# Gated mix of attention and mlp on one core: the mlp in 32-row tiles, in two phases

## The chip, the core and the metric

The kernel runs on 1 core of one Trainium2 chip. The metric is the device time of one execution in microseconds (us). Five engines work beside each other, each with its own queue that it goes through in order: TensorE (PE; its weight loads are listed as PEld), VectorE (DVE), ScalarE (ACT), GpSimd (POOL) and SyncE (SP), which here only starts transfers. Matrix products go to PSUM banks of 128 partitions x 512 float32 numbers.

## The reference

Attention and an mlp of the same input are mixed by a gate for each row; S = 2048 rows, D = 448 columns, 16 heads of 28, 1792 hidden columns, float32.

```python
qkv = (x @ wqkv).reshape(1, S, 3, 16, 28).transpose(2, 0, 3, 1, 4)
q, k, v = qkv
p = softmax(einsum("bhqd,bhkd->bhqk", q, k) * 28 ** -0.5)
a = einsum("bhqk,bhkd->bhqd", p, v).transpose(0, 2, 1, 3).reshape(1, S, D) @ wo
y = (x - mean(x)) / sqrt(var(x) + 1e-5)
b = gelu_tanh(y @ w1 + b1) @ w2 + b2
g = sigmoid((x * gate_w).sum(-1))
out = g * a + (1 - g) * b
```

## The kernel before

Float32 accuracy comes from splitting: a number is a high part (rounded to the type fp32r) and a low part, the difference, and a product is three matmuls: high x high, high x low, low x high. S is cut into NC = 4 chunks of CH = 512 rows or 16 tiles of 128 rows (TPC = 4 a chunk); heads into NG = 4 groups of four; the hidden columns into NF = 14 tiles of 128.

The stages run one after the other. First q, k and v are computed and stored to DRAM (qk holds high and low parts). Then comes the mlp, then attention, then the last projection and the output.

The mlp goes over s = c, f (chunk, hidden tile; line 400). `mlp1(c, f)` adds 11 matmuls of 128 rows into one bank ph (line 368: K is 448, padded to four tiles, the low part of y sharing the fourth), ACT applies the gelu twice (lines 373 and 374: rounded and not), POOL subtracts to get the low part hl (line 375). `mlp2` of the step before adds its three products into four banks, one for each 128 rows (lines 385, 386, 388), that live over all 14 hidden tiles. Finished rows go to DRAM (gbs). So PE alternates between 11 matmuls of 512 columns and 12 of 448.

Attention subtracts the row maximum of the scores. These maxima come from matmuls of their own: q and k high parts of one head stand in 28 of the 32 rows of a strip of TensorE's array, four heads in four strips (kd, qd). Each matmul (line 280) gives 128 x 512 scores, each is reduced by DVE (line 282); 1024 of them are needed. `Filler` spreads them: 394 between the mlp's matmuls, in groups of MG = 3, the others (aux) through attention. For every 64 a PE transpose (line 264) and a store to ms follow.

For attention, K tiles (`load_k`: one transfer of ones, line 331, and two of 224 KB, line 338) and q tiles (`load_q`) are started on SP's queue; the first 12 K tiles go into the space of the mlp's w1 tiles (ring kring, name w1f). Their start is written into the mlp loop, in chunk 3 behind f = 10. A slot of attention is one K tile of 128 rows against 512 rows of q for four heads: four score matmuls (line 528), two exponentials on ACT (line 531), then p times v of the slot before (line 536: four matmuls, each in its own strip of 32 columns of the array, with full float32 operands; the profile lists eight), and some row maxima. `finish` divides by the sums: the sums go out and back by POOL's queue (lt, rls, rc) and the projection is added to acc. Before that, POOL loads acc from gbs and scales it by 1 - g (lines 515, 517, 518).

The order in each queue is set by a scheduler that follows the program's order and the waits of each instruction; a transfer on SP may so be put ahead of or behind others.

Of the kernel before, what the change touches and what calls it, by code (L numbers as in the profile page):

```python
# [15 lines left out]
P = 128  # L16
# [14 lines left out]
MLP_MAX = 400  # L31
MG = 3
FS = 3
# [5 lines left out]
def kernel(ctx: ExitStack, tc: tile.TileContext, xt, wqk, wv, wo, xk, w1, b1, w2, b2,  # L39
# [18 lines left out]
    ms = [dram.tile([4, S], F32, name=f"ms{g}") for g in range(NG)]  # L58
# [11 lines left out]
    mpool = ctx.enter_context(tc.tile_pool(name="mpool", bufs=2, side="right"))  # L70

    aq = ctx.enter_context(tc.tile_pool(name="aq", bufs=1, side="right"))


    m0 = ExitStack()
    mw0 = m0.enter_context(tc.tile_pool(name="mw0", bufs=1, side="right"))
    my = m0.enter_context(tc.tile_pool(name="my", bufs=2, side="right"))

    w1h, w1l, w2h, w2l = {}, {}, {}, {}
    kring = []  # L80
    qring = [aq.tile([P, 4, CH], F32R, name=f"qst{i}") for i in range(3)]

    def load_w(f, pool1, pool, stage):
        r1 = stage.tile([P, 4, P], F32, name="r1")
        nc.sync.dma_start(r1, w1[f])
        t = pool1.tile([P, 8, P], F32R, name=f"w1f{f}")
        w1h[f], w1l[f] = t[:, 0:4], t[:, 4:8]
        if f >= 2:
            kring.append(t.rearrange("p a b -> p (a b)"))
        nc.scalar.activation(w1h[f], r1, AF.Copy)  # L90
        nc.gpsimd.tensor_sub(w1l[f], r1, w1h[f].bitcast(F32))
        r2 = stage.tile([P, D], F32, name="r2")
        nc.sync.dma_start(r2, w2[f])
        w2h[f] = pool.tile([P, D], F32R, name=f"w2h{f}")
        w2l[f] = pool.tile([P, D], F32R, name=f"w2l{f}")
        nc.scalar.activation(w2h[f], r2, AF.Copy)
        nc.gpsimd.tensor_sub(w2l[f], r2, w2h[f].bitcast(F32))

    yh, yl, lnr, lnx = {}, {}, {}, {}

    def ln_load(c, t):
        cs = slice(c * CH, (c + 1) * CH)
        if t == 0:
            lnr[c] = my.tile([P, 2, CH], F32, name="lnr", bufs=1)
            nc.sync.dma_start(lnr[c], lns.rearrange("(n t) i -> n (t i)", n=2)[:, cs].partition_broadcast(P))
        lnx[c, t] = my.tile([P, CH], F32, name="xr", bufs=4)
        nc.sync.dma_start(lnx[c, t], xt[t, :, cs])

    def ln_apply(c, t):
        if t == 0:  # L110
            yh[c] = qring[c % 2]
            yl[c] = my.tile([P, 3, CH], F32R, name="yl")
        x = lnx.pop((c, t))
        nc.vector.tensor_sub(x, x, lnr[c][:, 0])
        nc.gpsimd.tensor_mul(x, x, lnr[c][:, 1])
        nc.scalar.activation(yh[c][:, t], x, AF.Copy)
        if t < 3:
            nc.vector.tensor_sub(yl[c][:, t], x, yh[c][:, t].bitcast(F32))
        else:
            nc.vector.tensor_sub(yh[c][64:128, t], x[64:128], yh[c][64:128, t].bitcast(F32))  # L120


    with tc.tile_pool(name="qx", bufs=2) as qx, tc.tile_pool(name="qo", bufs=3) as qo, \
# [85 lines left out]
        for c in range(NC):  # L209
            for m in range(NM):  # L210
# [23 lines left out]
                if c == 2 and m in (3, 5):  # L234
                    load_w(m // 4, mw0, mw0, my)
                if c == 2 and m == 6 or c == 3 and m < 3:
                    ln_load(0, (m + 1) % 7)
                if c == 3 and m in (1, 2, 3, 4):
                    ln_apply(0, m - 1)
# [5 lines left out]
    def row_max(pool):  # L245

        kds, qds = {}, {}

        def load(n):
            g, c = divmod(n, NC)  # L250
            if c == 0:
                kds[g] = mpool.tile([P, S], F32R, name="kd")
                for j in range(4):
                    r = D + (4 * g + j) * DH
                    pool[1].dma_start(kds[g][32 * j:32 * j + DH].bitcast(F32), qk[0, r:r + DH])
            qds[n] = mpool.tile([P, CH], F32R, name="qd")
            for j in range(4):
                r = (4 * g + j) * DH
                pool[1].dma_start(qds[n][32 * j:32 * j + DH].bitcast(F32), qk[0, r:r + DH, c * CH:(c + 1) * CH])

        def close(n, mf):
            g, c = divmod(n, NC)
            ps = pool[0]()
            nc.tensor.transpose(ps[:4 * TPC, :P], mf, ident)
            mt = mpool.tile([4 * TPC, P], F32R, name="mt")
            nc.vector.tensor_scalar(mt, ps[:4 * TPC, :P], -1.0, None, op0=OP.mult)
            pool[1].dma_start(ms[g][:, c * CH:(c + 1) * CH].rearrange("j (i x) -> j i x", x=P), mt.bitcast(F32))

        load(0)
        last = None  # L270
        for n in range(NG * NC):
            kd, qd = kds[n // NC], qds[n]
            mx = mpool.tile([P, 4, TPC, 4], F32, name="mx")
            done = 0
            for i in range(TPC):
                for k in range(4):
                    for j in range(4):
                        ps = pool[0]()
                        r = slice(32 * j, 32 * j + DH)
                        nc.tensor.matmul(ps, qd[r, i * P:(i + 1) * P], kd[r, k * 512:(k + 1) * 512],  # L280
                                         start=True, stop=True)
                        nc.vector.reduce_max(mx[:, j, i, k:k + 1], ps, axis=AX)  # L282
                        done += 1
# [3 lines left out]
                        if done == 24 and n + 1 < NG * NC:  # L287
                            load(n + 1)
# [332 lines left out]
```

## Time and profile before

| what | us |
|---|---|
| time before, median of 2 runs | 1273.99 (1272.26 to 1275.72) |
| span of the profiled execution | 1271.2 |
| q, k, v, to about | 118 |
| mlp, from about 118 to | 503 |
| from the mlp's end until attention runs without a stop | 503 to 603 |
| attention | 603 to 1232 |
| last projection and output | 1232 to 1271.2 |

The profile is of one execution. A page gives busy times of the engines and the costliest groups of instructions; a timeline lists them one by one; windows give busy times for stretches; the chain of waits follows the end back to what it waited for. PE's ends are modelled: the distance from one start to the next says more than the length.

### The profile page before, as it was taken

The page shows a single profiled execution, that of the slowest core. Times are in us where ns is not written, and L with a number is a line of the kernel's source. Part 1 is how long each engine was busy: PE and PEld are TensorE (multiplying, and loading weights), DVE is VectorE, ACT ScalarE, POOL GpSimd, SP SyncE. Part 2 cuts the span into 40 slices and gives each one's busy share as a digit, 9 for nine tenths or more (in the row PEclk, how much of TensorE's full clock was granted, in tenths as well). Part 3 has the DMA queues.
Part 4 walks back from the last instruction along what each step waited for, and adds up shares of the span by engine and source line. Part 5 has one row for each costly group of instructions (what it writes and reads, how often), then busy time and mean ns, then how long its engine had stood idle before and what let it go on. Part 6 is the DMA issues. An engine that isn't in the chain of part 4 may idle for free.

```text
span 1271.2 us, 16167 instructions
## 1 busy us (share of the span) xinstructions
PE 1196.9 (94%) x6085; PEld 653.2 (51%) x6085; DVE 775.9 (61%) x1298; ACT 645.0 (51%) x765; POOL 322.5 (25%) x362
## 2 busy tenths in 40 slices
PE   7998999999999998196999999999999999999997
PEld 6886667766677665032444434444434444444433
DVE  3543377877776776144676757666756777676703
ACT  5243522212212211164677757767657767767784
POOL 4022952311222112356222121112022202211220
PEclk9999899999999999588999989999989999999998
DMA  8987740100101212532013142102412111210001
GB/s 281 295 279 261 203 108 25 46 9 1 37 16 47 72 53 82 147 112 59 17 40 75 53 103 78 38 10 56 99 64 61 44 31 38 76 35 34 25 24 58
DMA packets 56053, 101.44 MB, mean 80 GB/s; under 512 B 7352, under 2 KB 24240, under 8 KB 55528
## 3 DMA queue, kind: packets, MB, share of 16 engines
q1 hardware_dynamic: 41640, 82.53, 21.0%
q0 software_dynamic: 6016, 13.70, 4.0%
q10 hardware_dynamic: 8320, 4.19, 1.5%
q8 instruction: 48, 0.79, 0.3%
q14 instruction: 29, 0.24, 0.1%
HBM read 73.76 MB, written 26.49 MB: 79 GB/s over the span
## 4 chain that ended last, share of the span: by engine, by line
PE 75%; DMA 14%; POOL 5%; issue 2%; DVE 2%; ACT 1%; SPq 1%; ACTq 0%; POOLq 0%; DVEq 0%
PE sc L528 20%; PE pv L536 17%; PE ph L368 11%; PE aux L280 7%; PE pm L280 5%; PE acc L388 4%; PE acc L385 4%; PE acc L386 3%; DMA w1f<-qk 3%; DMA lt<-ob 2%; DMA xraw<-in_xt 2%; DMA acc<-gbs 2%; POOL acc L518 1%; PE ps L160 1%; PE aux L454 1%
## 5 line engine op out<-in xcount | busy, mean ns | idle before, releaser
L531 ACT ACTIVATE pt<-sc 128x1024 f32<-128x1024 f32 x512 | 496.5, 1021 | 230.6 <-PE sc L528 219.8
L282 DVE TENSOR_REDUCE mx<-aux 128x1 f32<-128x512 f32 x630 | 396.2, 683 | 176.8 <-PE aux L280 176.3
L528 PE MATMUL sc<-qst,w1f 113*128 113x512 f32 x1024 | 317.5, 429 | 33.9 <-ACT pt L531 33.9
L282 DVE TENSOR_REDUCE mx<-pm 128x1 f32<-128x512 f32 x394 | 248.1, 684 | 92.0 <-PE pm L280 91.6
L536 PE MATMUL pv<-pt,vg 128*32 128x512 f32 x2048 | 279.3, 617 | 0.0
L528 PEld LDWEIGHTS sc<-qst,w1f 113*128 113x128 f32 x1024 | 172.7, 191 | 152.5 <-ACT pt L531 83.6
L373 ACT ACTIVATE hh<-ph,b1s 128x512 fp32r<-128x512 f32 x56 | 38.4, 686 | 247.5 <-PE ph L368 247.5
L368 PE MATMUL ph<-qst,w1f 128*128 128x512 f32 x448 | 152.2, 413 | 7.1 <-ACT h L374 7.0
L280 PEld LDWEIGHTS aux<-kd,qd 28*128 28x128 f32 x630 | 45.0, 184 | 199.6 <-DVE mx L282 123.6
L375 POOL TENSOR_TENSOR hl<-h,hh 128x512 fp32r<-128x512 f32 x56 | 73.1, 1305 | 245.6 <-ACT h L374 244.3
L280 PE MATMUL aux<-kd,qd 28*128 28x512 f32 x630 | 116.7, 503 | 14.5 <-DVE mx L282 14.3
L368 PEld LDWEIGHTS ph<-qst,w1f 128*128 128x128 f32 x448 | 84.3, 192 | 34.3 <-issue 11.0
L536 PEld LDWEIGHTS pv<-pt,vg 128*32 128x32 f32 x2048 | 40.8, 108 | 92.5 <-issue 86.1
L388 PE MATMUL acc<-w2h,hl 128*128 128x448 f32 x224 | 87.2, 389 | 0.0
L385 PE MATMUL acc<-w2h,hh 128*128 128x448 f32 x224 | 84.5, 377 | 0.0
L386 PE MATMUL acc<-w2l,hh 128*128 128x448 f32 x224 | 82.0, 366 | 0.0
L465 POOL DMA_DIRECT2D lt<-ob x15 | 10.7, 716 | 254.3 <-DVE ob L464 254.3
L280 PE MATMUL pm<-kd,qd 28*128 28x512 f32 x394 | 73.5, 497 | 1.2 <-DVE mx L282 0.4
L368 PE MATMUL ph<-yl,w1f 128*128 128x512 f32 x168 | 69.5, 414 | 0.0
L455 DVE SCALAR_TENSOR_TENSOR acc<-aux,gate,acc 128x448 f32<-128x448 f32 x64 | 43.4, 678 | 39.3 <-PE aux L454 39.3
L280 PEld LDWEIGHTS pm<-kd,qd 28*128 28x128 f32 x394 | 28.2, 182 | 48.8 <-DVE mx L282 36.0
L160 PE MATMUL ps<-xh,wh 128*128 128x512 f32 x112 | 45.5, 406 | 7.0 <-ACT xh L147 6.4
(99 smaller groups left out, 980.8 us busy)
## 6 DMA issues: line engine op xcount, KB each, us to landing
qk<-hl SPq DMA_DIRECT2D x28, 512.0 KB
qst<-qk SPq DMA_DIRECT2D x64, 224.0 KB
w1f<-qk SPq DMA_DIRECT2D x64, 224.0 KB
xraw<-in_xt SPq DMA_DIRECT2D x16, 256.0 KB
vs<-vt SPq DMA_DIRECT2D x16, 256.0 KB
xr<-in_xt SPq DMA_DIRECT2D x16, 256.0 KB
rc<-rls POOLq DMA_DIRECT2D x60, 64.0 KB, 2.3
bxr<-in_xk SPq DMA_DIRECT2D x8, 448.0 KB
```

Source lines behind the costliest of these rows:

```text
L160: nc.tensor.matmul(ps, a, b, start=(i == 0), stop=(i == len(ops) - 1))
L280: nc.tensor.matmul(ps, qd[r, i * P:(i + 1) * P], kd[r, k * 512:(k + 1) * 512], start=True, stop=True)
L282: nc.vector.reduce_max(mx[:, j, i, k:k + 1], ps, axis=AX)
L368: nc.tensor.matmul(ps, a, b, start=(i == 0), stop=(i == len(ops) - 1))
L375: nc.gpsimd.tensor_sub(hl[c, f], h, hh[c, f].bitcast(F32))
L385: nc.tensor.matmul(a, hh[c, f][:, sl], w2h[f], start=(f == 0), stop=False)
L386: nc.tensor.matmul(a, hh[c, f][:, sl], w2l[f], start=False, stop=False)
L388: nc.tensor.matmul(a, hl[c, f][:, sl], w2h[f], start=False, stop=(f == NF - 1))
L455: nc.vector.scalar_tensor_tensor(acc[:, tt], po, gate[:, tt:tt + 1], acc[:, tt], op0=OP.mult, op1=OP.add)
L528: nc.tensor.matmul(ps[:, i], kst[g, j, h][:4 * DH + 1, kk * P:(kk + 1) * P], qst[g, c][:4 * DH + 1, j], start=True, stop=True)
L531: nc.scalar.activation(t, ps, AF.Exp, scale=SCALE)
L536: nc.tensor.matmul(pv[32 * j:32 * j + 32, :], vg[g][:, k, 32 * j:32 * j + 32], pt[j // 2][:, j % 2], start=(k == 0), stop=(k == NT - 1), s ...
```

## The change

The mlp is written anew. Every matmul of it has 32 rows, one strip of the array. An item of work, `Up` (one hidden tile of a chunk) or `Down` (one tile of 128 output rows), has one PSUM bank and passes through the strips in turn: an `Up` spends one step in each strip (42 matmuls in all), a `Down` four turns of the four strips (168 matmuls). In each step a new item may begin in strip 0, so that up to four are in flight, each in another strip and another bank; one round of a step is one matmul from each. There are 123 steps (`NC * (NF + 16) + 3`).

Where the banks move on by a strip, SP waits for the last matmul of each and increments the semaphore hand, and PE waits for that. Ahead of the wait PE has three row maxima (`visit`, into three banks with one reduction by DVE) and the first matmul of a new item.

In each chunk all 14 ups come first (steps 0 to 16 of 30), then the four downs (14 on): hidden values hh, hl are kept for all 14 tiles, one buffer each. w1 and w2 are loaded one tile per step in the first chunk. The order of all engines in this loop is fixed as it is written; attention's first loads (`attention_early`) start at step 108 (in the last chunk, one step after its last up is done), one K tile a step, into tiles of their own in the space of w1.

Row maxima: kd has one buffer instead of two, each strip is reloaded by itself; the transposes are 32 x 32 on DVE instead of PE; ms has another layout. 369 row maxima are done in the mlp, 655 in attention. Attention is otherwise as before, with a third q tile outside the ring of the mlp's.

```diff
-MLP_MAX = 400
-MG = 3
-FS = 3
...
-    ms = [dram.tile([4, S], F32, name=f"ms{g}") for g in range(NG)]
+    ms = [dram.tile([32, 4, 32], F32, name=f"ms{n}") for n in range(NG * NC)]
...
+    def split_w1(f, eng):
+        r = w1r.pop(f)
+        t = w1s[f] = w1p[0].tile([P, 7, P], F32R, name=f"w1f{f}")
+        lo = slice(64 * ((f + 1) % 2), 64 * ((f + 1) % 2) + 64)
+        nc.scalar.activation(t[:, 0:4], r, AF.Copy)
+        eng.tensor_sub(t[:, 4:7], r[:, 0:3], t[:, 0:3].bitcast(F32))
+        eng.tensor_sub(t[lo, 3], r[lo, 3], t[lo, 3].bitcast(F32))
...
+    yh = aq.tile([P, 4, CH], F32R, name="yh")
+    yl = aq.tile([P, 4, CH], F32R, name="yl")
...
+            self.kd = mpool.tile([P, S], F32R, name="kd")
+            self.qd = [mpool.tile([P, CH], F32R, name=f"qd{i}") for i in range(2)]
...
+        def load_k(self, g, j):
+            r = D + (4 * g + j) * DH
+            self.queue.dma_start(self.kd[32 * j:32 * j + DH].bitcast(F32), qk[0, r:r + DH])
...
+        def visit(self, ps, count):
+            self.flush()
+            first = self.m
+            count = min(count, 64 * NG * NC - first)
+            for b in range(count):
+                n, x = divmod(self.m, 64)
+                x, j = divmod(x, 4)
+                i, k = divmod(x, 4)
+                if x == 0 and n + 1 < NG * NC:
+                    self.load_q(n + 1, j)
+                r = slice(32 * j, 32 * j + DH)
+                nc.tensor.matmul(ps[:, b], self.qd[n % 2][r, i * P:(i + 1) * P], self.kd[r, k * 512:(k + 1) * 512],
+                                 start=True, stop=True)
+                if x == 15 and n % NC == NC - 1 and n + 1 < NG * NC:
+                    self.load_k(n // NC + 1, j)
+                self.m += 1
+            if count:
+                nc.vector.reduce_max(self.mx[:, first % 192:first % 192 + count], ps[:, :count], axis=AX)
+            if self.m // 64 > first // 64:
+                self.late.append(lambda: self.close(first // 64))
...
+            mf, mt = self.mf[n % 2], self.mt[n % 2]
+            mx = self.mx[:, 64 * (n % 3):64 * (n % 3) + 64].rearrange("p (i k j) -> p j i k", i=TPC, k=4)
+            nc.vector.reduce_max(mf[:, 0:16].rearrange("p (j i) -> p j i", j=4), mx, axis=AX)
+            nc.vector.tensor_scalar(mf[:, 0:16], mf[:, 0:16], -1.0, None, op0=OP.mult)
+            nc.vector.transpose(mt, mf)
+            def store():
+                self.queue.dma_start(ms[n].rearrange("c b x -> b c x"), mt)
+            self.later.append(store)
...
-        t = qring[(0, 2, 1)[nq % 3]]
+        t = qring[nq % len(qring)]
...
+    mp = m1.enter_context(tc.tile_pool(name="mp", bufs=5, space=PSUM, reuse_waits="tile"))
+    mr = m1.enter_context(tc.tile_pool(name="mr", bufs=1, space=PSUM, reuse_waits="tile"))
...
+    class Up:
+        def __init__(self, c, f):
+            self.c, self.f, self.phases = c, f, 4
+        def ops(self, n):
+            f, w = self.f, w1s[self.f]
+            r = slice(32 * n, 32 * n + 32)
             ops = []
             for t in range(3):
-                ops += [(w1h[f][:, t], yh[c][:, t]), (w1h[f][:, t], yl[c][:, t]), (w1l[f][:, t], yh[c][:, t])]
-            ops += [(w1h[f][:, 3], yh[c][:, 3]), (w1l[f][:, 3], yh[c][:, 3])]
-            for i, (a, b) in enumerate(ops):
-                nc.tensor.matmul(ps, a, b, start=(i == 0), stop=(i == len(ops) - 1))
-                filler.run(1, MG)
+                ops += [(w[r, t], yh[r, t]), (w[r, t], yl[r, t]), (w[r, 4 + t], yh[r, t])]
+            ops.append((w[r, 3], yh[r, 3]))
+            if n // 2 == f % 2:
+                ops.append((w[r, 3], yl[r, 3]))
+            return ops
+        def close(self):
+            f = self.f
             h = mh.tile([P, CH], F32, name="h", bufs=2)
-            hh[c, f] = mh.tile([P, CH], F32R, name="hh")
-            hl[c, f] = mh.tile([P, CH], F32R, name="hl")
-            nc.scalar.activation(hh[c, f], ps, AF.Gelu_apprx_tanh, bias=b1s[:, f:f + 1])
-            nc.scalar.activation(h, ps, AF.Gelu_apprx_tanh, bias=b1s[:, f:f + 1])
-            nc.gpsimd.tensor_sub(hl[c, f], h, hh[c, f].bitcast(F32))
-        acc2 = {}
-        def mlp2(c, f):
-            for i in range(TPC):
-                if f == 0:
-                    acc2[c, i] = mp2.tile([P, D], F32, name="acc2")
-                sl = slice(i * P, (i + 1) * P)
-                a = acc2[c, i]
-                nc.tensor.matmul(a, hh[c, f][:, sl], w2h[f], start=(f == 0), stop=False)
-                nc.tensor.matmul(a, hh[c, f][:, sl], w2l[f], start=False, stop=False)
-                filler.run(2, MG)
-                nc.tensor.matmul(a, hl[c, f][:, sl], w2h[f], start=False, stop=(f == NF - 1))
-                filler.run(1, MG)
-                if f == NF - 1:
-                    tt = c * TPC + i
-                    gb = mh.tile([P, D], F32, name="gb", bufs=2)
-                    if c < NC - 1:
-                        nc.scalar.activation(gb, a, AF.Copy)
-                    else:
-                        nc.vector.tensor_copy(gb, a)
-                    (nc.sync if c < NC - 1 else nc.gpsimd).dma_start(gbs[tt], gb)
-        prev = None
-        for s in range(NC * NF):
-            c, f = divmod(s, NF)
-            if c == 0 and f + 2 < NF:
-                load_w(f + 2, ak, mw, my)
-            if s == FS:
-                filler.spread(lambda: mp3.tile([P, 512], F32, name="pm"), nc.sync, MLP_MAX, (NC * NF - FS) * 23)
-            mlp1(c, f)
-            if prev is not None:
-                mlp2(*prev)
-            prev = (c, f)
-            if c == NC - 1 and f == 10:
-                for j in range(4):
-                    load_k(0, j, 0)
-                load_q(0, 0)
-                for j in range(4):
-                    load_k(0, j, 1)
-            if 1 <= f < 5 and c + 1 < NC:
-                ln_load(c + 1, f - 1)
-            if f >= 6 and f % 2 == 0 and c + 1 < NC:
-                ln_apply(c + 1, (f - 6) // 2)
-        mlp2(*prev)
-    m0.close()
+            nc.scalar.activation(hh[f], self.ps, AF.Gelu_apprx_tanh, bias=b1s[:, f:f + 1])
+            nc.scalar.activation(h, self.ps, AF.Gelu_apprx_tanh, bias=b1s[:, f:f + 1])
+            nc.gpsimd.tensor_sub(hl[f], h, hh[f].bitcast(F32))
+    class Down:
+        def __init__(self, c, i):
+            self.c, self.i, self.phases = c, i, 16
+        def ops(self, n):
+            v, s = divmod(n, 4)
+            r = slice(32 * s, 32 * s + 32)
+            sl = slice(self.i * P, (self.i + 1) * P)
+            cut = ((0, 11, 21, 32, 42), (0, 10, 21, 31, 42))[self.i % 2]
+            ops = []
+            for m in range(cut[v], cut[v + 1]):
+                f, p = divmod(m, 3)
+                ops.append(((hh, hh, hl)[p][f][r, sl], (w2h, w2l, w2h)[p][f][r]))
+            return ops
+        def close(self):
+            gb = mh.tile([P, D], F32, name="gb", bufs=2)
+            nc.scalar.activation(gb, self.ps[:, :D], AF.Copy)
+            nc.sync.dma_start(gbs[self.c * TPC + self.i], gb)
...
+    def extra(t):
+        c, x = divmod(t, NF + 16)
+        if c == 0:
+            if x + 3 < NF:
+                fetch_w1(x + 3)
+            if x + 2 < NF:
+                split_w1(x + 2, nc.gpsimd if x < 6 else nc.vector)
+            if 8 <= x < 8 + NF:
+                fetch_w2(x - 8)
+            if 9 <= x < 9 + NF:
+                split_w2(x - 9)
+        if c + 1 < NC:
+            if 20 <= x < 24:
+                ln_load(c + 1, x - 20)
+            if 22 <= x < 26:
+                ln_sub(c + 1, x - 22)
+            if 23 <= x < 27:
+                ln_split(c + 1, x - 23)
+    def attention_early():
+        m0.close()
+        ak = ctx.enter_context(tc.tile_pool(name="ak", bufs=1, side="right", reuse_waits="tile"))
+        kring.extend(ak.tile([P, 2 * CH], F32R, name=f"kst{i}") for i in range(NK))
+        for j in range(4):
+            load_k(0, j, 0)
+            yield
+        load_q(0, 0)
+        yield
+        for j in range(4):
+            load_k(0, j, 1)
+            yield
...
+    starts = {}
+    for c in range(NC):
+        for f in range(NF):
+            starts[c * (NF + 16) + f] = Up(c, f)
+        for i in range(TPC):
+            starts[c * (NF + 16) + NF + i] = Down(c, i)
+    hand = tc.alloc_semaphore("hand")
+    handed = 0
+    over = []
+    handoff = mybir.DependencyInfo(mybir.DependencyClass.Sync, mybir.DependencyReason.DATA)
+    with tc.manual_schedule():
+        rowmax.begin()
+        live = []
+        early = None
+        for t in range(NC * (NF + 16) + 3):
+            if t in starts:
+                starts[t].n = 0
+                live.append(starts[t])
+            if t == (NC - 1) * (NF + 16) + NF + 4:
+                early = attention_early()
+            if early is not None:
+                next(early, None)
+            todo = [[] for _ in range(4)]
+            for x in live:
+                s = x.n % 4
+                if x.n == 0:
+                    x.ps = mp.tile([P, CH], F32, name="acc")
+                ops = x.ops(x.n)
+                last = x.n == x.phases - 1
+                for m, (a, b) in enumerate(ops):
+                    todo[s].append((x, a, b, x.n == 0 and m == 0, last and m == len(ops) - 1))
+                x.n += 1
+            rowmax.visit(mr.tile([P, 3, 512], F32, name="pm"), 3)
+            if todo[0] and todo[0][0][3]:
+                x, a, b, st, sp = todo[0].pop(0)
+                nc.tensor.matmul(x.ps[:, :b.shape[-1]], a, b, start=st, stop=sp, skip_group_check=True)
+            if over:
+                sig = nc.sync.sem_inc(hand, 1)
+                for mm in over:
+                    tc.add_manual_dep(sig.ins, mm.ins.name, handoff, reason="handoff")
+                handed += 1
+                nc.tensor.wait_ge(hand, handed)
+                over = []
+            while any(todo):
+                for s in range(4):
+                    if not todo[s]:
+                        continue
+                    x, a, b, st, sp = todo[s].pop(0)
+                    n = b.shape[-1]
+                    mm = nc.tensor.matmul(x.ps[:, :n], a, b, start=st, stop=sp, skip_group_check=True)
+                    if not todo[s] and x.n < x.phases:
+                        over.append(mm)
+            for x in [x for x in live if x.n == x.phases]:
+                x.close()
+                live.remove(x)
+            extra(t)
...
-    filler.spread(aux, nc.gpsimd, NG * NC * 65, (NG * NC - 2) * NT + LQ - 1)
+    rowmax.queue = nc.gpsimd
+    qring.append(aw.tile([P, 4, CH], F32R, name="qst2"))
+    first, slots, slot = rowmax.m, (NG * NC - 2) * NT + LQ - 4, 0
...
-                filler.run(1, 3)
+                slot += 1
+                if rowmax.m == 1024:
+                    rowmax.flush()
+                if rowmax.m < 1024 and first + (1024 - first) * min(1, slot / slots) - rowmax.m >= min(3, 1024 - rowmax.m):
+                    for _ in range(3):
+                        if rowmax.m < 1024:
+                            rowmax.visit(aux().rearrange("p (b n) -> p b n", b=1), 1)
```

More of the change, by code (lines that the diff above doesn't have):

```diff
@@ L79 @@
[L79 to L97, printed above, removed]
@@ L295 @@
-    class Filler:
-        def __init__(self):
-            self.pool = [None, None]
-            self.it = row_max(self.pool)
-            self.first = self.upto = self.slot = self.done = 0
-            self.slots = 1
-        def spread(self, pool, queue, upto, slots):
-            self.pool[:] = pool, queue
-            self.first, self.upto, self.slots, self.slot = self.done, upto, slots, 0
-        def run(self, n=1, group=1):
-            self.slot += n
-            due = self.first + (self.upto - self.first) * min(1, self.slot / self.slots) - self.done
-            group = min(group, self.upto - self.done)
-            if due >= group:
-                for _ in range(group):
-                    next(self.it, None)
-                    self.done += 1
@@ L321 @@
+    rowmax = RowMax()
     HS = S // 2
@@ L424, in sb @@
+    m1.close()
     def sb(name, bufs):
```

138 lines of the change are left out of this document (65 added, 73 removed).

## The prediction

> **What bounds the kernel now.** The page comes first: who is busy, and how long the execution was.
>
> ```profile
> span 1271.2 us, 16167 instructions
> PE 1196.9 (94%) x6085; PEld 653.2 (51%) x6085; DVE 775.9 (61%) x1298; ACT 645.0 (51%) x765; POOL 322.5 (25%) x362
> ```
>
> TensorE (PE) looks like the only bound, but 94% is an average over stages, so the windows come next (columns: stretch, length, busy time of PE, PEld, DVE, ACT, POOL, granted clock, DMA share, GB/s).
>
> ```profile
> 170.00:503.00 333.00, 333.00 (x1530) 232.58 (x1530) 245.19 (x399) 74.22 (x120) 77.82 (x68) 1.00 0.13 40
> 503.00:545.00 42.00, 8.09 (x28) 3.10 (x30) 4.73 (x11) 6.55 (x8) 15.34 (x16) 0.58 0.52 143
> 545.00:603.00 58.00, 46.82 (x260) 17.87 (x252) 29.75 (x49) 33.61 (x35) 35.44 (x31) 0.88 0.30 82
> 603.00:1232.00 629.00, 623.35 (x3473) 261.92 (x3473) 413.92 (x686) 438.88 (x453) 118.62 (x179) 0.98 0.19 51
> ```
>
> The mlp (to 503 us) and the attention (from 603 us) leave PE no gap. Between them lies a hole of two halves, and the change touches both sides of it. The chain of waits says what made it (start, length, what):
>
> ```profile
> 507.65 33.24 DMA w1f<-qk
> ...
> 550.70 10.42 DMA acc<-gbs
> 561.19 2.25 POOL acc L517 x2
> ...
> 597.48 2.72 POOL acc L518 x2
> 600.20 2.22 DMA lt<-ob
> ...
> 603.30 1.98 PE aux L280 x3
> ```
>
> First the K tiles of attention have to land, about 541 us; then PE does some twenty attention slots until it needs the first division, whose small transfer (lt) stands on POOL behind the initialisation of acc from the stored mlp rows: 561 to 600 us. So a shorter mlp is worth its gain only if K loads and that POOL chain also come earlier. Their order decides this case.
>
> **Part 1, the matmuls.** PE's timeline in the middle of the mlp (start, length, group):
>
> ```profile
> 299.65 0.39 PE L368 MATMUL ph<-qst,w1f 128*128 128x512 f32 x1
> 299.88 0.40 PE L368 MATMUL ph<-yl,w1f 128*128 128x512 f32 x1
> ...
> 302.15 0.86 PE L368 MATMUL ph<-qst,w1f 128*128 128x512 f32 x3
> 302.94 0.50 PE L280 MATMUL pm<-kd,qd 28*128 28x512 f32 x3
> 303.37 0.47 PE L385 MATMUL acc<-w2h,hh 128*128 128x448 f32 x1
> 303.68 0.37 PE L386 MATMUL acc<-w2l,hh 128*128 128x448 f32 x1
> 303.88 0.36 PE L388 MATMUL acc<-w2h,hl 128*128 128x448 f32 x1
> ```
>
> Starts are 0.23 us apart at 512 columns and 0.20 us at 448. Three row maxima, on three strips at once, hold the next full matmul off for 0.43 us (302.94 to 303.37), and that one takes 0.31 instead of 0.20 (to 303.68); before them 302.15 + 3 x 0.23 = 302.84, 0.10 us early. A triple costs 0.43 + 0.11 + 0.10 = 0.64 us, and of 394 row maxima there are 131 triples: 84 us of the mlp.
>
> The Trainium skill's page "TensorEngine Tiling (Array Packing)", section Key Properties, says that changing the tiling mode drains TensorE; the 0.43 and 0.31 us agree, and by that rule an mlp in 32-row tiles throughout pays no drain at a triple.
>
> After the change a step has 10 or 11 rounds of four strip matmuls. Strip matmuls: 56 ups x 42 and 16 downs x 42 x 4, together 5040, or 1260 rounds where there were 616 + 672 = 1288 full matmuls: the stream saved is only 28 x 0.22 = 6 us, if a round goes at the cadence of one full matmul. No row of before shows four row strips back to back. The near bound is 0.23 us (a strip reads only its own 32 partitions); the far one the four-wide packing by columns:
>
> ```profile
> 552.44 1.06 PE L536 MATMUL pv<-pt,vg 128*32 128x512 f32 x8
> 553.43 0.50 PE L280 MATMUL aux<-kd,qd 28*128 28x512 f32 x3
> ```
>
> Eight of these take 0.99 us, 0.50 us a round of four. There each strip pulls its own 128-partition stream, where row strips share one, and the operands are full float32 instead of fp32r. So I take 0.23, and keep 0.50 as the far end.
>
> **Part 2, the hand-over.** At each of 122 steps PE waits until the last matmul on every bank is done, by way of SP. What such a wait costs is bounded by how late ACT sees a bank finished, and by a wait's own length on PE's queue:
>
> ```profile
> 303.05 0.69 ACT L373 ACTIVATE hh<-ph,b1s 128x512 fp32r<-128x512 f32 x1 [5.01 <-PE ph L368]
> L528 PEldq EVENT_SEMAPHORE  x54: 51/51/1697, 499.4 to 1215.8; - x54
> ```
>
> The last ph starts at 302.15 + 2 x 0.23 = 302.61, ACT at 303.05: 0.44 us. With two hops of 51 ns, 0.54 us from the last round's start to the next round's; the row-max triple and one first matmul lie inside. With 11 rounds a step is 10 x 0.23 + 0.54 = 2.84 us (up) or 10 x 0.20 + 0.54 = 2.54 us (down). From below: without the wait 11 x 0.23 = 2.53. From above: another 0.4 us for SP, 3.2.
>
> Does something else bound a step? One reduction covers three banks:
>
> ```profile
> L282 DVE TENSOR_REDUCE mx<-pm x394: 669/681/694, 143.7 to 500.5; 128x1 f32<-128x512 f32 x197
> L375 POOL TENSOR_TENSOR hl<-h,hh 128x512 fp32r<-128x512 f32 x56 | 73.1, 1305 | 245.6 <-ACT h L374 244.3
> ```
>
> Three at 0.68 are 2.04 us if nothing is shared; the next triple waits for it, and 0.53 + 2.04 = 2.57 fits the step, barely in the down phase. POOL has 1.3 us per up beside weight splits; its cover is thin only in the first steps.
>
> The count: 17 up steps and 13 down-only steps a chunk. K loads are released when the last up is done, after 107 steps: 68 x 2.84 + 39 x 2.54 = 292 us. The first step now begins with row maxima, whose kd loads are late on SP:
>
> ```profile
> 127.40 0.41 SPq L255 DMA_DIRECT2D kd<-qk  x1
> ...
> kd<-qk POOLq DMA_DIRECT2D x8, 224.0 KB, 4.3
> ```
>
> 127.4 + 4.3 = 131.7 at the latest, so 131 (the mlp began about 118 before). kd has one buffer now: a strip is reloaded when its last reader is done and is wanted a step later, 4.3 against 2.8 us, twice over: +5 us once in the mlp. The ups are done at S = 131 + 292 + 5 = 428 us.
>
> **Part 3, K loads and SP's queue.** SP's own timeline before:
>
> ```profile
> 423.57 0.25 SPq L331 DMA_DIRECT2D w1f<-ones  x1
> ...
> 478.07 6.93 SPq L331 DMA_DIRECT2D w1f<-ones  x1
> 485.05 4.66 SPq L338 DMA_DIRECT2D w1f<-qk  x2
> 489.81 6.30 SPq L331 DMA_DIRECT2D w1f<-ones  x1
> 496.16 5.05 SPq L338 DMA_DIRECT2D w1f<-qk  x2
> ```
>
> An SP transfer waits for an earlier one to land: 489.81 - 478.07 = 11.7 us a K tile. Twelve tiles took 423.6 to 541 = 117 us, and would again, so K is complete at S + 117 = 545 us, hardly later than before. The cost is what stands behind: SP also carries the hand-overs, one a step, between the K tiles. In the compiled order the ones of the last 7 steps stand behind tile 7, and the last three of these behind stores of mlp rows that wait in turn for transfers four from the end. Four at 4.67 are 19 us (a half tile: 24 in 112 us, by a stretch of K loads alone, 224 KB at 50 GB/s)
>
> ```profile
> 702.00:724.00 22.00, 22.00 (x130) 9.76 (x129) 15.58 (x26) 14.98 (x16) 0.86 (x1) 1.00 0.13 50
> ```
>
> so the mlp ends at E = 545 - 19 + 5 = 531 us instead of 428 + 16 x 2.6 = 470: it ends later than before (503), for all the work that it saves.
>
> **Part 4, what follows E.** acc is loaded after the mlp and initialised in 16 pairs of 1.1 and 1.4 us: 10.4 + 40 = 50 us (550.70 to 600.20, with two waits for later loads within), plus a few for weights of the projection: E + 58 to E + 83, 589 to 614 us; middle 602, where before had 603. PE itself: K landed at 545, and the twenty slots of 2.55 us end at 551 + 30 to 531 + 51 = 582: the POOL chain still ends last. In attention: 25 more row maxima at 0.14 us (+4), no transposes (-4), and the single kd buffer at two changes of group, 5 us each, on a PE that has no gap: +10.
>
> Sum, on the profiled time: 1271.2 - 1 + 10 = 1280 us; the median lies 1273.99 - 1271.2 = 2.8 above: 1283. Its own range, by the step (2.5 to 3.2: -33 to +39 us at S, and K, E and the chain move with S) and the chain (+-12), taken as independent: 1248 to 1324.
>
> **Rivals.**
> *A: the hand-overs are not held* (SP issues ahead of the landings). For: the first eight transfers need not wait. Against: the 4.7 to 6.9 us rows. Then E = 470, the POOL chain is done by 553, and PE waits for K alone: 545 + 30 = 575, 28 us earlier: 1255; with a step of 2.5 us as well, 1222.
>
> *B, slower: PE can't issue that fast.* A round is eight instructions (four weight loads, four matmuls) in 0.23 us, 29 ns each. The windows show 2 x 1530 in 333 us, 109 ns, and the eight-matmul group of pv 16 in 0.99 us, 62 ns. At 40 ns a round is 0.32 us and a step 0.9 us longer: S + 96, 1283 + 96 = 1379; at 62 ns, +290, 1573. It decides from 29 ns on. That the three of a triple start together (302.94, one row) speaks against, for a burst.
>
> *C: rounds slow by packing.* At 0.30 us: +0.7 us a step, 107 steps, +75: 1358; at the columns' 0.50, +290.
> The Trainium skill's page "TensorE: Matmul & The Clock Gate", section Measured speedup vs the span model, gives four row tiles of K=32, N=512 as 3.07 times, not 4: by that, as an estimate, 4 x 0.23 / 3.07 = 0.30 us a round, rival C. It speaks against this change; that speedup looks like one burst's, fill included, and no run here shows a stream.
>
> *D: it doesn't do what it says*, that is, strips do not overlap: 0.93 us a round, +880 us. The triples contradict it.
>
> **How the numbers follow.** Forecast 0.55, A 0.15, B 0.13, C 0.15, D 0.02. Within its own range the forecast has 0.08 below 1248.5, 0.32 between, 0.15 above 1299.5 (2% to either side of 1273.99, about what a measurement of this kernel can tell from no change). A splits 0.12 faster, 0.03 same; B to D are slower but for 0.01. A step shorter than all bounds here (rounds that run on through the hand-over, strip by strip) would move part of the forecast to faster: 0.05 from same. Faster 0.25, same 0.31, slower 0.44. For 8 in 10 the range leaves out half of A below and the far ends of B and D above: 1235 to 1375.
>
> **What would show it.** Right: PE cadence of 0.23 us in fours; steps of 2.8 us; SP with waits of 4 to 7 us on K from about 430 us and PE idle behind SP in the same stretch; the mlp's last matmul near 531; POOL's acc chain ending near 600. Wrong: PE done with the mlp near 470 (A); even gaps of 40 ns or more between PE's instructions (B); rounds of 0.3 us (C). If the ups end much before 428 us, the whole tail moves with them.

## The result, and the profile after

The changed kernel takes 1336.77 us (median of 2 runs, 1336.39 to 1337.14), against 1273.99 before: 1.0488 times, 95% interval 1.0447 to 1.0528. It is slower by 63 us. The profiled execution has a span of 1335.3 us, 64.1 more than before.

First the windows of the changed kernel, cut where its stages end (columns as in the prediction: stretch, length, busy time of PE, PEld, DVE, ACT, POOL, granted clock, DMA share, GB/s). From 651.8 us on attention runs without a stop; below this moment is called its restart.

```profile
260.00:300.00 40.00, 39.87 (x673) 35.78 (x670) 27.53 (x19) 11.91 (x19) 12.93 (x10) 1.00 0.14 45
457.90:582.50 124.60, 57.85 (x615) 47.59 (x611) 26.37 (x15) 1.63 (x3) 1.85 (x3) 0.66 0.18 64
582.50:651.80 69.30, 62.06 (x285) 23.64 (x284) 34.52 (x62) 40.81 (x43) 52.37 (x49) 0.77 0.45 124
651.80:1335.30 683.50, 660.55 (x3644) 279.02 (x3644) 440.48 (x736) 459.55 (x480) 125.24 (x188) 0.96 0.18 51
```

The mlp itself is dense: 39.87 of 40 us in its middle. From the first step behind the last up that is held (step 108, 457.9 us) to the last matmul of the mlp 125 us pass, for work that took 45 us when nothing held it (the run with K on POOL's queue, below); PE is busy for less than half of them. The waits of that stretch name the cause (engine, line waited for, total us, times, longest):

```profile
PE acc L490 <- SPq L478: 66.7, 12, 13.9
PEld acc L490 <- SPq L478: 64.6, 13, 14.4
```

Line 478 is the increment of the semaphore hand, on SP. SP's timeline shows what stands ahead of it there:

```profile
472.67 4.73 SPq L338 DMA_DIRECT2D kst<-qk  x2
477.44 4.87 SPq L331 DMA_DIRECT2D kst<-ones  x1
482.36 4.72 SPq L338 DMA_DIRECT2D kst<-qk  x2
487.20 3.57 SPq L331 DMA_DIRECT2D kst<-ones  x1
...
505.36 9.04 SPq L348 DMA_DIRECT2D yh<-qk  x4
514.91 1.75 SPq L350 DMA_DIRECT2D yh<-ms  x1
...
552.91 4.72 SPq L338 DMA_DIRECT2D kst<-qk  x2
570.52 13.65 SPq L406 DMA_DIRECT2D gbs<-gb  x4
```

and PE's timeline the other side of two of these waits (in brackets the idle time before the instruction, and what ended it):

```profile
487.20 0.74 PE L490 MATMUL acc<-w2h,hl 32*128 32x448 f32 x1 [13.42 <-SPq L478]
505.36 0.73 PE L490 MATMUL acc<-w2l,hh 32*128 32x448 f32 x1 [13.95 <-SPq L478]
```

PE starts again at 487.20 and at 505.36, the moments at which SP begins its next transfer: the increment went out just ahead of it. The row maxima of step 108 start at 457.9 us and those of step 117 at 561.7: nine steps in 104 us, where nine of 2.6 us would take 23.

The hand-over in the dense part, in PE's timeline:

```profile
302.68 0.37 PE L490 MATMUL acc<-w2h,hh 32*128 32x448 f32 x2
302.70 0.36 PE L490 MATMUL acc<-w2l,hh 32*128 32x448 f32 x1
302.72 0.36 PE L490 MATMUL acc<-w2h,hh 32*128 32x448 f32 x1
302.89 0.36 PE L490 MATMUL acc<-w2l,hh 32*128 32x448 f32 x1
302.89 0.38 PE L297 MATMUL pm<-kd,qd 28*128 28x512 f32 x1
302.90 0.36 PE L490 MATMUL acc<-w2h,hl 32*128 32x448 f32 x1
302.93 0.36 PE L490 MATMUL acc<-w2l,hh 32*128 32x448 f32 x1
303.11 0.42 PE L297 MATMUL pm<-kd,qd 28*128 28x512 f32 x2
303.39 0.47 PE L490 MATMUL acc<-w2h,hh 32*128 32x448 f32 x4
303.70 0.36 PE L490 MATMUL acc<-w2l,hh 32*128 32x448 f32 x4
```

Four matmuls of a round start within some 40 ns, the next round 0.20 us later (302.68, 302.89): four strips in the time of one full matmul. Where the banks move on, a strip that has no matmul left (302.89) takes a row maximum at once, and the next round starts at 303.39, 0.46 us after the last matmul (302.93).

The beginning of the mlp is the second place that lost time. DVE's timeline there:

```profile
170.88 1.74 DVE L303 TENSOR_REDUCE mx<-pm 128x3 f32<-128x1536 f32 x1
175.77 1.23 DVE L87 TENSOR_TENSOR w1f<-st,w1f 128x384 fp32r<-128x384 f32 x1 [3.15 <-ACT w1f L86]
177.02 1.12 DVE L88 TENSOR_TENSOR w1f<-st,w1f 64x128 fp32r<-64x128 f32 x1
178.17 1.76 DVE L303 TENSOR_REDUCE mx<-pm 128x3 f32<-128x1536 f32 x1
```

The reduction of a step's row maxima stands on DVE behind the split of a weight tile (lines 87 and 88), the split waits for ACT's copy (3.15 us idle), and ACT's copy stands behind the gelu of the step before. The next step's row maxima wait for that reduction (PE starts them at 179.98, after 3.23 us of waiting). The first 14 steps take 64.6 us (row maxima of step 0 at 122.3, of step 14 at 186.9) instead of 14 x 2.84 = 40.

### The profile page after: what moved, and what is told of

It reads as the page before. It is cut to its first block, busy times and chain, and to the rows that moved or that the text cites. A ratio compares the mean times of both kernels' runs of the same rounds, so it can differ in the third digit from the quotient of the medians.

```text
span 1335.3 us, 23564 instructions
## 1 busy us (share of the span) xinstructions
PE 1205.1 (90%) x9821; PEld 711.8 (53%) x9821; DVE 762.7 (57%) x1062; ACT 648.1 (49%) x769; POOL 336.1 (25%) x377
## 5 line engine op out<-in xcount | busy, mean ns | idle before, releaser
L303 DVE TENSOR_REDUCE mx<-pm 128x3 f32<-128x1536 f32 x123 | 216.0, 1756 | 206.9 <-PE pm L297 165.0
L490 PE MATMUL acc<-w2l,hh 32*128 32x448 f32 x896 | 178.4, 397 | 23.0 <-SPq L478 22.9
L490 PE MATMUL acc<-w2h,hl 32*128 32x448 f32 x896 | 171.4, 394 | 21.4 <-SPq L478 21.4
L490 PE MATMUL acc<-w2h,hh 32*128 32x448 f32 x880 | 162.8, 401 | 25.4 <-SPq L478 25.4
L490 PE MATMUL acc<-yh,w1f 32*128 32x512 f32 x1512 | 183.9, 412 | 0.2 <-POOL w1f L87 0.2
L490 PE MATMUL acc<-yl,w1f 32*128 32x512 f32 x784 | 161.4, 408 | 8.4 <-SPq L478 8.4
L490 PEld LDWEIGHTS acc<-w2l,hh 32*128 32x128 f32 x896 | 117.9, 201 | 33.3 <-SPq L478 30.8
L490 PEld LDWEIGHTS acc<-yh,w1f 32*128 32x128 f32 x1512 | 129.5, 192 | 7.9 <-POOL w1f L87 1.2
L490 PEld LDWEIGHTS acc<-w2h,hl 32*128 32x128 f32 x896 | 116.7, 201 | 28.1 <-SPq L478 16.3
L606 PE MATMUL sc<-yh,kst 113*128 113x512 f32 x384 | 124.4, 445 | 1.6 <-ACT pt L609 1.6
```

What stands on the lines that cost most here:

```text
L303: nc.vector.reduce_max(self.mx[:, first % 192:first % 192 + count], ps[:, :count], axis=AX)
L490: mm = nc.tensor.matmul(x.ps[:, :n], a, b, start=st, stop=sp, skip_group_check=True)
L606: nc.tensor.matmul(ps[:, i], kst[g, j, h][:4 * DH + 1, kk * P:(kk + 1) * P], qst[g, c][:4 * DH + 1, j], start=True, stop=True)
```

## The experiments

The theory after this reading: the loss is queueing. (1) SP's hand-over increments stand behind attention's K loads; (2) DVE's reductions stand behind weight splits; the strips themselves work as intended. The rivals: the strips or the row-max triple cost time in every step; K transfers slow the matmuls; or what follows (K, POOL's chain) ends as late whatever the mlp does. Later a third part came up: (3) kd, with one buffer, stops attention. A variant without a range was executed once; the kernel before spread from 1271.6 to 1278.4 us beside these runs.

**K loads on ACT's queue.** Both K and the first two q tiles leave SP:

```diff
+        eng = nc.scalar if nk < NK else nc.sync
...
-            nc.sync.dma_start(t[r:r + 2 * DH].bitcast(F32), src)
+            eng.dma_start(t[r:r + 2 * DH].bitcast(F32), src)
```

> The changed kernel, with attention's first 12 K tiles and first two q tiles started on ACT's queue instead of SP's, so that SP's hand-over increments have no K load ahead of them. Theory (the hand-overs of steps 108 to 116 are late because they queue behind K loads on SP): steps 108 to 122 go back to 2.5 to 2.9 us, the mlp's last matmul is near 500 us instead of 580, and the time is 1280 to 1300 us, not less, because K itself still lands 117 us after the last up and the copies of the last mlp rows now stand behind K loads on ACT. Rival (the late steps are slow because K transfers slow the matmuls' data or the banks are not free): steps 108 to 116 stay at 9 us or more and the time stays above 1325.

Measured: 1330.08 us. Steps 108 to 120 go back to 2.6 us each (row maxima at 458.5 and 490.0), as the theory said; but then PE stands from 490.6 to 563.1, and the mlp ends at 577.8. The queues of ACT and SP say why:

```profile
554.17 7.89 ACTq L339 DMA_DIRECT2D kst<-qk  x2
562.11 0.54 ACT L407 ACTIVATE gb<-acc 128x448 f32<-128x448 f32 x1 [104.41 <-issue]
```

```profile
562.68 16.66 SPq L408 DMA_DIRECT2D gbs<-gb  x4
```

ACT's copy of the first finished mlp rows now stands behind the last K load, the store of these rows on SP behind the copy, and the last hand-overs behind the store. The wait was moved, not removed: the effect on the steps is shown, the time that was forecast (1280 to 1300) was missed, because the chain through the store was overlooked.

**Splits ahead of the gelu.** One line is moved:

```diff
+            extra(t)
             for x in [x for x in live if x.n == x.phases]:
                 x.close()
                 live.remove(x)
-            extra(t)
```

> The changed kernel, with each step's loads and weight splits written ahead of the gelu of the step's finished up, instead of behind it. Theory (in the first 14 steps DVE's reduction stands behind a weight split, that behind ACT's copy, and that behind the gelu, which waits for the end of the step): steps 4 to 13 go from 4.3 us on average to about 3, the last up ends 15 to 25 us earlier (430 to 440 us instead of 455), all later stages shift by that, and the time is 1310 to 1322. Rival (the weights arrive too late from memory, or POOL's splits are the limit): steps 4 to 13 stay above 4 us and the time above 1328.

Measured: 1332.19 us. Step 14 begins at 176.1 instead of 186.9, and the ups are done 11 us earlier, all of it from the first steps. So the order on ACT and DVE was 11 of the 25 us; three steps still take 3.8 to 4.4 us, and the first four over 4 us each, as in the changed kernel. The mlp ends 11 us earlier too (571.2 instead of 582.6), and attention restarts at 640.0 instead of 651.8. The total follows by only 4.6 us, so the forecast (1310 to 1322) was missed: attention took 690.4 us here instead of 683.5. How far that part varies is told below.

**No row maxima in the mlp** (it leaves out the mlp's row-max matmuls and reductions, and attention uses zeros for them):

```diff
-            rowmax.visit(mr.tile([P, 3, 512], F32, name="pm"), 3)
+            rowmax.visit(None, 3)
```

> The changed kernel without the 369 row maxima of the mlp, matmuls and reductions both (their loads and stores stay); the maxima used for these rows are zeros. Theory (a row-max triple lies inside the wait for the hand-over and costs next to nothing): the steady step shrinks from 2.77 us by less than 0.2; the first 14 steps lose their lock with DVE and go from 64 to under 50 us; the late steps 108 to 116 stay at 9 us or more. Rival (a triple costs its 0.43 us of TensorE in every step): the steady step is 2.35 us or less, 40 us over the mlp.

Measured: 1319.6 us. ACT's timeline gives the step, by the first gelu of every up; first the changed kernel, then this one:

```profile
254.77 0.69 ACT L382 ACTIVATE hh<-acc,b1s 128x512 fp32r<-128x512 f32 x1 [1.78 <-PE acc L490]
...
260.31 0.69 ACT L382 ACTIVATE hh<-acc,b1s 128x512 fp32r<-128x512 f32 x1 [1.74 <-PE acc L490]
```

```profile
237.63 0.69 ACT L384 ACTIVATE hh<-acc,b1s 128x512 fp32r<-128x512 f32 x1 [1.85 <-PE acc L492]
...
243.16 0.69 ACT L384 ACTIVATE hh<-acc,b1s 128x512 fp32r<-128x512 f32 x1 [1.80 <-PE acc L492]
```

Two steps take 5.54 us with row maxima and 5.53 without. A triple is free where banks move on; before the change it had cost some 0.64 us. The rival is out. The gain of 17 us lies ahead of the steady part: the fourteenth up is done 16.6 us earlier (gelu at 179.4 instead of 196.0 us). The late steps are held as before, with gaps of 3 to 14 us on PE and the mlp's end at 563.9.

**K tiles 8 to 11 moved.** These four tiles belong to the second group of heads and are needed 160 us later.

```diff
         for j in range(4):
             load_k(0, j, 1)
             yield
+        for j in range(4):
+            load_k(1, j, 0)
```

> The changed kernel, with K tiles 8 to 11 (of the second group of heads) written behind the mlp loop, so that they no longer stand between the hand-overs; tiles 0 to 7 stay there. Theory: eight half tiles of 4.67 us go from ahead of the hand-overs, 37 us: the mlp's last matmul near 543 us instead of 580, the time 1295 to 1305. Rival (not the number of K loads ahead but something else sets the late steps): last matmul later than 570, time above 1325.

Measured: 1356.21 us, 19 more. The expectation says that the tiles stand behind the mlp loop; in the program as it was built they stood in step 117, all four ahead of the last hand-overs, and PE stood for 31.6 us there (531.0 to 562.7). So the run does not test what it was meant to. It does show a K load ahead of a late hand-over costing about as much as one ahead of an early one: the mlp's last matmul starts at 586.1 us instead of 582.6. Of the 19 us, 13 lie in attention (696.2 us instead of 683.5), and their cause stays open. The test was made again, with the tiles tied to a score matmul of attention:

```diff
+                if g == 0 and c == 1 and k % 2 and k < 8:
+                    load_k(1, k // 2, 0, lastsc[0])
```

> The changed kernel with K tiles 8 to 11 on SP only after a score matmul of the second chunk of rows; tiles 0 to 7 and q on SP between the hand-overs as in the changed kernel. Theory (the wait is proportional to the K loads that stand ahead): steps 108 to 122 shrink by eight half tiles of 4.67 us, 30 to 40 us, the mlp ends near 543 us, the time is 1292 to 1305. Rival (the hold is all or nothing): the mlp ends later than 570 us, the time is above 1325.

Measured: 1310.56 us. The mlp's last matmul starts at 549.4 us instead of 582.6: 33 us for eight half tiles, 37 by the sum. The hold is not all or nothing; it grows with the loads that stand ahead. The total fell by 26 us, less than the 32 to 45 that were forecast.

**K loads on POOL's queue**, which has no other work in these steps, and tiles 8 to 11 late as in the last run:

```diff
+        eng = nc.gpsimd if nk < 8 else nc.sync
...
-            nc.sync.dma_start(t[r:r + 2 * DH].bitcast(F32), src)
+            eng.dma_start(t[r:r + 2 * DH].bitcast(F32), src)
```

> The changed kernel with the K tiles 0 to 7 and the first q tile of attention started on POOL's queue, and tiles 8 to 11 (second group of heads, needed 160 us later) on SP only after a score matmul of the second chunk of rows. SP's increments, the stores of the last mlp rows and ACT's loads of v then have no K load ahead of them. Theory (the changed kernel's loss is the queueing behind K loads): steps 108 to 122 take 2.5 to 2.9 us, the mlp ends at 495 to 505 us, tile 7 lands near 545, attention runs without a stop from 575 to 595 instead of 652, and the time is 1250 to 1282. Rival (with the hold gone the chain on POOL or K itself ends as late as before): above 1300.

Measured: 1265.62 us, 71 less than the changed kernel. The windows from the last up to the end of the mlp, the restart and the end:

```profile
457.00:495.00 38.00, 36.41 (x597) 31.41 (x596) 24.61 (x14) 1.09 (x2) 18.76 (x32) 1.00 0.61 143
495.00:574.00 79.00, 60.48 (x303) 25.66 (x298) 36.89 (x63) 41.25 (x44) 52.65 (x49) 0.83 0.43 121
574.00:1264.00 690.00, 667.89 (x3644) 281.93 (x3644) 440.72 (x736) 459.59 (x480) 124.99 (x188) 0.95 0.19 52
```

All traffic together, the transfers of K tiles 0 to 7 in it, now runs at 143 GB/s beside matmuls at a granted clock of 1.00, PE is busy for 36.41 of 38 us, and the mlp's last matmul starts at 501.5 us. K transfers do not slow the matmuls; only the queue did. Attention runs without a stop from 573.8 instead of 651.8. The run before had the late tiles alone, so the other queue is worth some 45 of the 71 us. On POOL the profile also names what a K load waits for, the landing of an earlier one:

```profile
465.79 0.51 POOL L332 DMA_DIRECT2D kst<-ones  x1 [3.05 <-DMA kst<-qk]
```

> The same as the run before it, and each step's loads and weight splits ahead of the gelu. Theory: the 11 us that this took from the first 14 steps, which the wait for K swallowed when it was tried alone, now count: 8 to 13 us less than the run before it. Rival: still swallowed, less than 4.

With the splits first as well: 1251.44 us, 14.2 less, a little more than expected; 7.4 of them are there at the restart (566.4 instead of 573.8), the rest in attention. Executed four times, beside the kernel before:

> The kernel of the run with K tiles on POOL's queue and the splits first, timed in rounds against the kernel before. Theory: 1248 to 1255, 1.5 to 2% under the kernel before. Rival: a single good run; 1260 or more.

Measured: 1253.50 us (1250.89 to 1254.79), 0.982 times the kernel before, 95% interval 0.9796 to 0.9844.

**Attention.** From its restart to the end the profiled execution takes 651.8 to 1335.3 = 683.5 us in the changed kernel, 603.3 to 1271.2 = 667.9 before. The variants so far lie between 680 and 696 (K on ACT 680.1, on POOL 690.0, then 683.3 and 681.9 with the splits first), those of the kernel before at 668 to 671. So a difference of some 7 us between two variants of one kernel says little here, and 12 to 15 between the two kernels does. PE's timeline in the changed kernel, where the row maxima go on to the fourth group of heads:

```profile
1005.58 1.07 PE L614 MATMUL pv<-pt,vg 128*32 128x512 f32 x8
1009.31 0.76 PE L297 MATMUL aux<-kd,qd 28*128 28x512 f32 x1 [2.67 <-issue]
1012.87 0.76 PE L297 MATMUL aux<-kd,qd 28*128 28x512 f32 x1 [2.80 <-DMA kd<-qk]
1014.08 0.76 PE L297 MATMUL aux<-kd,qd 28*128 28x512 f32 x1 [0.45 <-DMA kd<-qk]
```

PE waits for kd, strip by strip, and so it does, for less, where they go on to the third group (748.5 us). The test is a second buffer for the third group, loaded 60 row maxima ahead:

```diff
+    rowmax.kds[2] = aw.tile([P, S], F32R, name="kd2")
```

> The same with a second kd buffer in attention (the third group's; the fourth goes back to the first), loaded 60 row maxima ahead instead of strip by strip at the change of group. Theory (of the 15 us by which the changed kernel's attention is longer, single-buffered kd costs 10): the gaps of PE at the two changes of group go, 8 to 11 us less than the run beside it, 1238 to 1246. Rival (the 25 row maxima more and their reductions are the cost): less than 4 us.

Measured: 1245.02 us (1242.50 to 1246.74), 0.9752 times the kernel before (0.9723 to 0.9781). PE's gaps at both changes of group are gone, and from the restart it takes 574.8 to 1243.9 = 669.1 us, below all variants with one buffer and within 1.2 of the kernel before, although it has 25 row maxima more. But POOL started the early loads of kd ahead of the first division's transfer, and there PE stood for longer:

```profile
574.75 1.98 PE L297 MATMUL aux<-kd,qd 28*128 28x512 f32 x3 [19.57 <-DVE mx L304]
```

> The run with two kd buffers, its loads tied to the row-max matmul beside which they are written, so that POOL no longer starts them ahead of the first division's small transfer (there PE stood for 19.6 us instead of 6). Theory: 6 to 12 us less, 1233 to 1240. Rival: the transfers cost the same wherever they stand, less than 3 us.

With these loads tied to their row maxima: 1242.12 us (1241.66 to 1242.78), 0.9741 times (0.9717 to 0.9765). That wait fell to 9.84 us, and the restart came 10 us earlier, but the ratio hardly moved: 0.9741 and 0.9752 cannot be told apart (the two ran on different chips), so the rival's "less than 3 us" came out. Attention then takes 564.5 to 1240.7 = 676.2 us, with a new wait of 4.30 us for K of the third group at 901 us. Why K came later there stays open.

**The kernel before with K tiles 8 to 11 late**, by the same lines:

> The kernel before, with only K tiles 8 to 11 put later (on SP after a score matmul of the second chunk of rows), all else as it was, row maxima and mlp too. Theory: these eight half tiles of 4.67 us stood ahead of what attention waits for, so the hole from 503 to 603 us shrinks by 20 to 37 us and the time is 1237 to 1258. Rival (POOL's chain behind the end of the mlp sets the restart): 1268 or more.

> The kernel before with K tiles 8 to 11 late, beside the last variant of the changed kernel on the same chip: what the old mlp gives once its K loads are ordered. Theory (the mlp in strips is itself worth its 6 to 11 us a chunk once nothing else waits): 1255 to 1265, so 15 to 30 us more than the variant with strips. Rival: the two within 8 us of each other.

Measured: 1260.57 us in one run, a little above the forecast, then 1255.21 (1254.36 to 1256.13), 0.9844 times (0.9824 to 0.9865). The restart of attention comes at 584.9 to 587.6 us instead of 603.3, still set by POOL's chain. Beside it on the same chip the mlp in strips, with all its queues put right, is 13.1 us faster, a little under what was expected: its mlp ends 15 us earlier and its attention takes 8 us longer. The mlp of before was not run with K on POOL's queue, so what the strips alone are worth is not shown.

## Why the prediction was right or wrong

Its range held the time, and its largest chance was on slower; its likeliest value, 1283 us, was 54 too low, and the range of that case alone (to 1324) did not hold it. By its own steps:

- *Rounds at the cadence of one full matmul*: right (0.20 us apart in fours). Rivals B, C and D are out: eight instructions per round were issued in 0.20 us. The Trainium skill's page "TensorE: Matmul & The Clock Gate", section Measured speedup vs the span model, gives 3.07 times for four row tiles. This trace has a stream of them at about 4 times (a round of four in the 0.20 us that one full matmul took before; 0.23 at 512 columns), and the measurement decides.
- *Hand-over of 0.54 us, steps of 2.84 and 2.54*: right: 0.46 in the rows above, 5.54 for two steps with ups, 2.6 for steps with downs alone. That the triple lies inside was shown by leaving it out.
- *The ups are done at 428*: 455 in fact. Mis-sized: the first 14 steps cost 25 us more. Of these, 14 lie in steps 4 to 13 (42.6 us instead of 28.4). The prediction noticed that POOL's cover is thin there, and did not price the order on DVE and ACT; moving the splits gave back 11 of the 14. The other 11 lie in steps 0 to 3 (22 us instead of 11.4): PE waits 3.1 us for qd, and then its rounds are slow without a gap, at a granted clock of 0.57, which the prediction had put at nothing:

```profile
132.00:144.00 12.00, 12.00 (x93) 9.38 (x95) 5.15 (x3) 1.91 (x2) 1.58 (x3) 0.57 0.21 65
```

The start itself came 9 us earlier than forecast (122.3 instead of 131), and the later steps took 11 more, much of it 1 us in each of four steps where a chunk begins.

- *The hand-overs are held by K loads on SP, so that the mlp ends later than before*: right in kind, shown by the runs with K on ACT, on POOL, and with fewer K loads ahead. Mis-sized: 125 to 127 us from the last up instead of 103. The sum had 61 us of waiting and 42 of work. PE's own waits for the hand-overs come to 66.7 us, 6 more, although the sum had K tiles only and the q tile among them takes 9.04 + 1.75 us on SP. The work between them took 60 us, 18 more: in the window its granted clock is 0.66, and behind the waits PE's rounds run 0.37 us apart. By PE's rows most of what was missing is slower work, and not more waiting; whether faster rounds would only have waited longer is not shown.
- *From the mlp's end to the restart, 58 to 83 us*: 69, right by size, and POOL's chain ended last, as forecast. DVE had copied the first sums (ob) by 642.4 us; POOL was still scaling acc until 647.8, put two loads of qd ahead, and started the transfer of the sums (lt) at 648.8. PE, done with its slots at 649.0, waited for it:

```profile
641.71 0.69 DVE L540 COPY ob<-pv 128x512 f32<-128x512 f32 x1 [0.33 <-PE pv L614]
644.99 2.78 POOL L594 TENSOR_SCALAR acc<-acc,ngate 128x448 f32<-128x448 f32 x2
648.78 0.72 POOL L541 DMA_DIRECT2D lt<-ob  x1
651.84 1.98 PE L297 MATMUL aux<-kd,qd 28*128 28x512 f32 x3 [2.79 <-DVE mx L303]
```

In the other variants with single kd, too, the restart comes 69 to 73 us behind the mlp's last matmul, and PE waits there for 6 to 10 us. What the prediction had too short is PE's own way to this point: 66 us instead of 51, because its first slots were slow. Without that, PE would have waited longer for the same chain:

```profile
604.91 2.08 PE L606 MATMUL sc<-yh,kst 113*128 113x512 f32 x4
...
609.51 2.08 PE L606 MATMUL sc<-yh,kst 113*128 113x512 f32 x4
...
613.82 1.20 PE L606 MATMUL sc<-yh,kst 113*128 113x512 f32 x4
616.38 1.19 PE L606 MATMUL sc<-yh,kst 113*128 113x512 f32 x4
```

A slot of 4.60 us at 605, of 2.56 from 614 on; the window from 580 to 620 has a granted clock of 0.58.

- *Attention 10 us longer*: 15.6 in fact; two kd buffers took it to 669.1 in one variant and 676.2 in the next, against 681.9 in the run beside the first. So most of it is the single kd; its share is known to some 7 us.

The errors add up: 27 + 24 - 2 + 6 = 55 = 1335.3 - 1280.

## What to carry to other kernels

A signal that an engine waits for in every step should not share an in-order queue with bulk transfers: each transfer that must wait for an earlier landing delays every signal behind it. When such a queue is relieved, follow the whole chain (copy, store, next signal) to see where the wait moves to. And an engine order that is fixed by hand puts a short operation that the next step needs behind a long wait just as easily: what the next step waits for is written first.

## What the runs showed of the hardware that was not expected

While the K loads held SP, all traffic together came to 64 GB/s (457.9 to 582.5 us); with K tiles 0 to 7 on POOL's queue it was 143 GB/s (457 to 495 us). The share of busy DMA engines in these rows is 0.18 and 0.61; why the second is faster stays open.

Behind the idle stretches PE's granted clock was 0.58 to 0.66, and rounds took longer; in the run without the waits the same matmuls had a clock of 1.00. Behind the wait that ends at 487.20 us the rounds were 0.37 us apart until 490.35, and 0.20 at 490.81. The last rounds of the mlp in the changed kernel, in PE's timeline:

```profile
582.25 0.57 PE L490 MATMUL acc<-w2l,hh 32*128 32x448 f32 x1
582.62 0.57 PE L490 MATMUL acc<-w2h,hl 32*128 32x448 f32 x1
```

They are 0.37 us apart, where the dense part has 0.20. The waits so cost twice here: the time itself, and slower rounds behind it. That idle time is what lowers the clock is not shown: from 132 to 144 us it was 0.57 while PE had no gap.
